# A two-layer GELU network with its gradients on one core: three moves in the order of TensorE's products

## The chip, the cores and the metric

The kernel runs on one core of one Trainium2 chip. The metric is the device time of one execution in microseconds; the time before is 266.73 us, the median of 3 runs (266.65 to 266.77). Profiles are of one execution each. The engines are TensorE (PE, matrix products; PEld is its loading of weights), VectorE (DVE), ScalarE (ACT), GpSimd (POOL) and SyncE (SP, which only issues transfers here).

## The reference

The forward pass of a dense layer, a GELU and a second dense layer, and the gradients of all five inputs for a given gradient of the output, in bf16 with S = 2048 rows, D = 448 and F = 1792:

```python
B, S, D, F = 1, 2048, 448, 1792
def _fwd_reference(x, w1, b1, w2, b2):
    h = jnp.einsum("bsd,df->bsf", x, w1) + b1
    h = _gelu(h)                                # tanh form
    return jnp.einsum("bsf,fd->bsd", h, w2) + b2

def reference(x, w1, b1, w2, b2, grad_out):
    _out, _vjp = jax.vjp(_fwd_reference, x, w1, b1, w2, b2)
    return (_out, *_vjp(grad_out))
```

## The kernel before

**Names.** u is x·w1 + b1 before the GELU, h the GELU of it, q = grad_out·w2ᵀ (the gradient that reaches h), gh = q times the slope of the GELU. All of them are held transposed, F on the partitions. An output row tile ("unit") is either of kind o, h·w2 + b2 for 128 rows, or of kind x, gh·w1ᵀ for 128 rows, the gradient of x. The gradients of the weights are xᵀ·gh (w1) and hᵀ·grad_out (w2), that of the biases are sums over rows.

**Tiling.** The 2048 rows are four blocks of 512, F is seven pairs of two 128-wide tiles, so there are 28 steps (block, pair). A step makes u for a pair (`PU[f]`, two PSUM banks), later q for a pair (`PQ[k]`, a pair of banks), and in between ScalarE and VectorE work out h and gh. D = 448 is three full tiles of 128 and a rest of 64. A unit is 14 products of 128 rows by 448 columns, summed over F.

**Two halves of the array.** From the third u on, nearly all products are made by `half_product` (line 265) as products of 64 rows: `side_by_side` issues them in pairs, one on the lower and one on the upper 64 rows of the array, into two different banks. Each pair of full tiles is thus gone through twice: once with the lower rows of the one bank and the upper rows of the other ("first half"), then the other way round ("second half"). When a bank is taken up by the other half of the rows, `half_product` makes TensorE wait until the last product of the first half on that bank is done, unless an earlier wait covers it. `u_of` and `q_of` give the six products of a half, `u_tail` and `q_tail` the products with the rest of 64 rows, `units_side(uns, second, tiles)` the unit products of two units side by side: two for each tile, 28 for all.

**The stages.** (1) The first u's with full 128-row products (L244, L505), after 11 warm-up products (L190). (2) Single steps i = 1 to 11 (the loop at line 556): each issues the u of step i+2, the q of step i, and slices of units between their halves, in the order that the list `between` gives. u of every single step goes into banks 0 and 1 (`open_u`), which ScalarE's `copy_u` (L345) must have emptied before. (3) Double steps, n = 0 to 7 (the loop at line 646): each takes two q's (ks) and prepares two u's (nxt). On TensorE it issues the rests of the u's and q's (`pe_tails`), then `pe_q_rows` (the six-product groups of both q's and the first half of the odd u), then what the diff changes: the first half of the even u around the first half of two units, then the second half of the units, then the second halves of both u's. On VectorE it issues the GELU's slope (`dve_gate`) with the evictions of finished units in the middle of it, then gh (`dve_gh`, L403); on ScalarE the tanh (L363), evictions of x units (L441), copies of u, square (L354) and GELU (L351). (4) The last units (to 177 us). (5) The weight gradients: w1's full tiles (`gw1_full`, L782, 128x128 of the array), w1's rests (`gw1_tail`, L793: two column halves of the array, 128x64), then w2's (`gw2_tile`, L814, 128x128).

**What sets the order.** The program is written in a manual schedule: each engine executes its instructions in the order in which the functions issue them; semaphores between engines are added from the reads and writes of the tiles. PSUM has eight banks: four single ones (`order_a`) and two pairs, two0 and two1. In the double steps q of an even number opens in two0 and of an odd number in two1 (`open_q`), and the two units of a step open in two1 (`open_two(1, 2)`) once gh has read the odd q from there. They must be evicted (`evict`: VectorE L443 for o, ScalarE L441 for x, then a store issued by GpSimd) before the next odd q opens, and `pe_tails` of the next step starts with that odd q, each q product behind a u rest.

Of the kernel before, what the change touches and what calls it, by code (L numbers as in the profile page):

```python
# [19 lines left out]
def kernel(  # L20
# [180 lines left out]
    def cols(p, a):  # L201
        return slice((2 * FP[p] + a) * P, (2 * FP[p] + a + 1) * P)
# [105 lines left out]
    def side_by_side(one, other, part=slice(0, None)):  # L308
        for lo, hi in list(zip(one(LOW), other(HIGH)))[part]:
            half_product(*lo)  # L310
            half_product(*hi)

    def u_of(f, a, first=False):
        b, p = divmod(f, NPAIR)
        return lambda hf: [(("u", f, a), PU[f][a][:], w1_f[hf, kt, cols(p, a)], xT[b][hf, kt, :], hf, first and kt == 0, False)
                           for kt in range(KF)]
# [206 lines left out]
    uns = [open_units[0:2], open_units[2:4]]  # L523
# [6 lines left out]
    def two_units(banks):  # L530
        for n in banks:
            open_unit(one_bank(n, "ps")[:, 0:D])
        return open_units[-2:]

    def fill(part):
        if isinstance(part, tuple):
            part = [(part[0], part[1], t) for t in part[2]]
        for uns, second, t in part:
            units_side(uns, second, [t])

    def tiles(p):
        return range(2 * p, 2 * p + 2)
# [12 lines left out]
    act_gelu([2])  # L555
    for i in range(1, NSINGLE):
        f = i + LEAD
        if i < 6:
            between = [(uns[1], False, tiles(i)), (uns[0], True, tiles(i)[:1]), (uns[0], True, tiles(i)[1:]), (uns[1], True, tiles(i))]
        elif i == 6:  # L560
            between = [(uns[0], True, tiles(i)), (uns[1], False, tiles(i)[:1]), (uns[1], False, tiles(i)[1:]), (uns[1], True, tiles(i))]
        else:
            if i == 7:
                ahead, later = xs, two_units((2, 3))
                slots = [(ahead, False, t) for t in range(6, NF - 2)] + [(later, False, t) for t in range(4)]
                slots += [(ahead, False, t) for t in range(NF - 2, NF)] + [(later, False, t) for t in range(4, NF)]
                slots += [(ahead, True, t) for t in range(NPAIR)] + [(later, True, t) for t in range(NF)]
                slots += [(ahead, True, t) for t in range(NPAIR, NF)]
            between = [slots[2 * c:2 * c + 2] for c in range(5)]
            del slots[0:10]  # L570
        open_u(f)
        open_q(i)
        if i == 1:
            fill(between[0])
        side_by_side(u_of(f, 0, True), u_of(f, 1, True))
        if i > 1:
            fill(between[0])
        else:
            fill(between[1])
        side_by_side(u_of(f, 1), u_of(f, 0))  # L580
        if i > 1:
            fill(between[1])
        pe_tail_pair(f, i, 1)
        pe_tail_pair(f, i, 0)
        fill(between[2])
        side_by_side(q_of(i, 0), q_of(i, 1))
        fill(between[3])
        side_by_side(q_of(i, 1, True), q_of(i, 0, True))
        if i < 6:
            units_side(uns[0], False, tiles(i + 1))  # L590
        elif i > 6:
            fill(between[4])
        if i > 1:
            act_tanh([i])
        if i == 6:
            evictions(2)
        copy_u(f, "aa")
        if i == NSINGLE - 1:
            evictions(2)
        act_square([f])  # L600
        if i == NSINGLE - 1:
            evictions()
        act_gelu([f])
        if i == 1:
            dve_chain("both 1", "cubic 2", "gate 1", "cubic*u 2", "slope 2", "gh 1", "slope*h 2", "cubic 3")
        elif i < NSINGLE - 1:
            dve_chain(f"both {i}", f"cubic*u {i + 1}", f"gate {i}", f"slope {i + 1}", f"gh {i}", f"slope*h {i + 1}", f"cubic {f}")
        else:
            dve_chain(f"both {i}", f"cubic*u {i + 1}", f"gate {i}", f"slope {i + 1}", f"slope*h {i + 1}", f"gh {i}",
                      f"cubic {f}", f"cubic*u {f}", f"slope {f}", f"slope*h {f}")  # L610
        if i == 6:
            evictions()
            open_two(1, 2)
            xs = open_units[-2:]
            units_side(xs, False, range(0, 6))
        if i == 9:
            nc.gpsimd.dma_start(out=g_low[0:DL, :], in_=gT[1][DL:P, 0, :])
            g_swap[1] = g_low
        if i < 8 or i % 2:
            traffic(i if i < 8 else (i + 7) // 2)  # L620
        if i > 6:
            stores(2, f - 1)
# [23 lines left out]
    for n in range(nq):  # L646
        i = 10 + n
        k = NSINGLE + 2 * n
        ks = [k, k + 1]
        fs = [k + 2, k + 3] if k + 2 < NSTEP else []  # L650
        nxt = [k + 4, k + 5] if k + 4 < NSTEP else []
        if n == 0:
            evictions()
        act_tanh(ks)
        if n > 0:
            dve_gate(ks, evictions)
        if n == 0:
            pe_u_rows(fs)
        if fs:
            pe_tails(fs if n == 0 else fs[::-1], ks[::-1])  # L660
        for f in fs[::-1]:
            copy_u(f, "aa")
        pe_q_rows(ks, nxt)
        if n == 0:
            a_ = part_a(ks)
            nc.vector.tensor_scalar(out=a_, in0=a_, scalar1=1.0, scalar2=math.sqrt(0.5), op0=ALU.add, op1=ALU.mult)
            dve_chain(f"tanh {k + 1}", f"gate {k + 1}", f"tanh {k}", f"gh {k + 1}", f"gate {k}", f"gh {k}")
        else:
            for q in ks[::-1]:
                dve_gh(q)  # L670
        ahead = 1 if n else 2
        if nxt:
            open_u(nxt[0])
            side_by_side(u_of(nxt[0], 0, True), u_of(nxt[0], 1, True), slice(0, ahead))
            open_two(1, 2)
            uns = open_units[-2:]
            units_side(uns, False)
            side_by_side(u_of(nxt[0], 0, True), u_of(nxt[0], 1, True), slice(ahead, None))
            units_side(uns, True)
            side_by_side(u_of(nxt[1], 1), u_of(nxt[1], 0))  # L680
            side_by_side(u_of(nxt[0], 1), u_of(nxt[0], 0))
        elif fs:
            uns, held = two_units(order_a[2:4]), two_units(order_a[0:2])
            units_side(uns, False)
            units_side(held, False)
            pe_tails([], [k + 2, k + 3])
            units_side(uns, True)
        if fs:
            act_square(fs)
            act_gelu(fs)  # L690
            dve_cubic(fs)
        if i == 15:
            nc.gpsimd.dma_start(out=g_low[DL:P, :], in_=gT[3][0:DL, 0, :])
            g_swap[3] = g_low
        traffic(i)
        stores(3, k + 1)
# [4 lines left out]
    for banks in (order_a[2:4], None, order_a[0:2], order_a[2:4]):  # L701
        if banks is None:
            open_two(0, 2)
            uns = open_units[-2:]
        else:
            uns = two_units(banks)
# [81 lines left out]
    def gw1_tail(ft0, n):  # L788
        ps = bank_w()
        for st_ in range(NS):  # L790
            b, j = PLACE[st_]
            for h in range(2):
                nc.tensor.matmul(ps[h * DL:(h + 1) * DL, 0:n * P], lhsT=x_nat[:, st_, KF * P:D],  # L793
                                 rhs=gh_nat[:, b, ft0 + h * n:ft0 + (h + 1) * n, j, :], start=(st_ == 0), stop=(st_ == NS - 1),
                                 tile_position=(0, h * DL), skip_group_check=True)
        o = stg.tile([P, SB], BF16, name="st", tag="st")
        nc.scalar.copy(out=o[:, 0:n * P], in_=ps[:, 0:n * P])
        for h in range(2):
            t0, t1 = ft0 + h * n, ft0 + (h + 1) * n
            while t0 < t1:  # L800
                t2 = t0 + 1
                while t2 < t1 and f_at(t2) == f_at(t2 - 1) + P:
                    t2 += 1
                c0 = (t0 - ft0 - h * n) * P
                queued.append(nc.scalar.dma_start(out=out_2[KF * P:D, f_at(t0):f_at(t0) + (t2 - t0) * P],
                                                  in_=o[h * DL:(h + 1) * DL, c0:c0 + (t2 - t0) * P]))
                t0 = t2

    def gw2_tile(ft, halves):
# [8 lines left out]
            queued.append(nc.scalar.dma_start(out=out_4[ft * P:(ft + 1) * P, h * w:(h + 1) * w], in_=o[:, 0:w]))  # L818
        return done

    for ft0, n in ((0, 4), (4, 4), (8, 4), (12, 2)):
        for kt in range(KF):
            gw1_full(ft0, n, kt)
            emit_sum(3)
        if ft0 == 12:
            gw1_tail(0, 4)
            gw1_tail(8, 3)
    for ft in range(NF):
        last = gw2_tile(ft, 2 if ft == NF - 1 else 1)
        if ft + 4 < NF:  # L830
# [35 lines left out]
```

## Time and profile before

| | |
|---|---|
| median of 3 runs | 266.73 us |
| the profiled execution, its time | 267.09 us |
| its span, first to last instruction | 265.3 us |
| TensorE products | 2171, busy 261.6 us |
| VectorE, ScalarE, GpSimd busy | 174.8, 137.4, 42.7 us |
| single steps, i = 1 to 11 | about 14.7 to 67.4 us |
| double steps, n = 0 to 7 | about 67.8 to 153 us |
| weight gradients | 177.2 to 262.5 us |

TensorE's share of busy time is an upper view, since a product's end is modelled and consecutive products overlap in the records; the starts of the products tell how fast they follow each other. A line of the timeline gives start, duration, engine, line of the kernel, operation, output <- inputs, shape and count; instructions that follow each other are merged into one line with their count. "[0.72 <-PE ps L265]" behind a line is the idle time of the engine before it and what ended it. A product of 64 rows is shown as 64*128.

### The profile page before, as it was taken

To read this page: it belongs to the slowest core of one execution; us is meant where nothing else is said; L and a number is where in the kernel's file an instruction comes from. 1 tells how busy PE (TensorE), PEld (TensorE's weight loads), DVE (VectorE), ACT (ScalarE), POOL (GpSimd) and SP (SyncE) were. 2 spreads that over 40 slices of the span, in tenths; PEclk is the share of its full clock that TensorE was granted. 3 is DMA by queue.
4 is the path that set the end of the run, shared out by engine and by line. 5 is a ranking of instruction groups with operands and counts; after the bars stand their busy time and mean duration, and the time that the engine had idled before them with its cause. 6 is when DMAs were issued, how large, how long until landed. Compare 5 with 4: busy or idle time off the path is not lost.

```text
span 265.3 us, 5207 instructions
## 1 busy us (share of the span) xinstructions
PE 261.6 (99%) x2171; PEld 148.9 (56%) x2171; DVE 174.8 (66%) x217; ACT 137.4 (52%) x164; POOL 42.7 (16%) x54
## 2 busy tenths in 40 slices
PE   8999999999999999999999999999999999999995
PEld 3444444444466565555658888864444765555554
DVE  1599999999998978769897731129999991000000
ACT  2799997887997686877749410022111111121111
POOL 1003003300302021010311111220700008900000
PEclk9999999999999999999999999999999999999999
DMA  7999999999999999465381359999211102999851
GB/s 177 234 239 197 215 216 153 227 101 259 282 220 193 248 206 268 89 171 110 95 161 49 67 125 308 349 164 276 81 40 40 49 22 56 212 216 224 203 129 35
DMA packets 111511, 44.47 MB, mean 168 GB/s; under 512 B 91104, under 2 KB 110272, under 8 KB 111488
## 3 DMA queue, kind: packets, MB, share of 16 engines
q1 hardware_dynamic: 104256, 35.79, 65.3%
q0 software_dynamic: 1984, 4.65, 7.2%
q10 hardware_dynamic: 5248, 3.71, 4.7%
q8 instruction: 17, 0.28, 0.4%
q14 instruction: 6, 0.05, 0.1%
HBM read 7.23 MB, written 14.23 MB: 81 GB/s over the span
## 4 chain that ended last, share of the span: by engine, by line
PE 99%; ACT 0%; issue 0%
PE ps L265 32%; PE ps_v L814 16%; PE pu L265 16%; PE pq L265 15%; PE ps_w L782 14%; PE ps_w L793 2%; PE pw L190 2%; PE pu L244 2%; PE pu L505 0%; PE ps L431 0%; ACT st L817 0%
## 5 line engine op out<-in xcount | busy, mean ns | idle before, releaser
L265 PE MATMUL pq<-gT,w2T 64*128 64x512 bf16 x386 | 55.6, 376 | 0.0
L265 PE MATMUL ps<-w_sb,hT 64*128 64x448 bf16 x440 | 49.0, 349 | 0.0
L265 PE MATMUL ps<-w1T_sb,ghT 64*128 64x448 bf16 x448 | 48.8, 349 | 0.0
L345 ACT ACTIVATE U<-pu,b1T 128x512 bf16<-128x512 f32 x54 | 33.5, 688 | 18.9 <-PE pu L265 14.4
L814 PE MATMUL ps_v<-g_nat,h_nat 128*128 128x448 bf16 (+1 forms) x240 | 42.6, 340 | 0.0
L403 DVE SCALAR_TENSOR_TENSOR ghT<-AZ,pq 128x1024 bf16<-128x1024 bf16 x28 | 33.9, 1218 | 12.3 <-PE pq L265 11.8
L265 PE MATMUL pu<-xT,w_f 64*128 64x512 bf16 x300 | 41.4, 376 | 0.0
L444 POOL DMA_DIRECT2D out_dram<-st x32 | 19.8, 625 | 133.3 <-DVE st L443 70.9
L265 PEld LDWEIGHTS <-ghT 64*128 64x128 bf16 x448 | 28.9, 94 | 15.3
L782 PE MATMUL ps_w<-gh_nat,x_nat 128*128 128x512 bf16 (+1 forms) x192 | 36.5, 352 | 0.0
L265 PEld LDWEIGHTS <-hT 64*128 64x128 bf16 x440 | 26.4, 94 | 17.0 <-issue 0.5
L265 PEld LDWEIGHTS <-w2T 64*128 64x128 bf16 x392 | 26.4, 94 | 14.9 <-PE pq L265 1.0
L814 PEld LDWEIGHTS <-h_nat 128*128 128x128 bf16 x240 | 23.3, 98 | 19.3 <-DMA out_dram<-st 0.3
L363 ACT ACTIVATE AZ<-AZ 128x1024 bf16<-128x1024 bf16 (+1 forms) x20 | 27.8, 1391 | 6.8 <-DVE AZ L359 6.8
L768 DVE TENSOR_TENSOR acc<-acc,gh_nat 128x1792 f32<-128x1792 f32 x14 | 30.0, 2142 | 0.5
L782 PEld LDWEIGHTS <-x_nat 128*128 128x128 bf16 x192 | 18.7, 98 | 17.9 <-issue 0.4
L354 ACT ACTIVATE AZ<-U 128x1024 bf16<-128x1024 bf16 (+1 forms) x21 | 28.2, 1342 | 0.9 <-DVE U L347 0.4
L351 ACT ACTIVATE hT<-U 128x1024 bf16<-128x1024 bf16 (+1 forms) x22 | 28.0, 1277 | 0.0
L817 ACT CAST st<-ps_v 128x448 bf16<-128x448 f32 (+1 forms) x15 | 7.6, 507 | 34.8 <-PE ps_v L814 34.8
L265 PEld LDWEIGHTS <-w_f 64*128 64x128 bf16 x300 | 16.2, 94 | 15.0 <-issue 0.7
L441 ACT CAST st<-ps 128x448 bf16<-128x448 f32 x16 | 7.8, 539 | 29.3 <-PE ps L265 27.6
L785 ACT CAST st<-ps_w 128x512 bf16<-128x512 f32 (+1 forms) x12 | 6.4, 532 | 27.7 <-PE ps_w L782 27.7
(58 smaller groups left out, 192.2 us busy)
## 6 DMA issues: line engine op xcount, KB each, us to landing
hT_dram<-hT SPq DMA_DIRECT2D x28, 256.0 KB, 3.2
out_dram<-st POOLq DMA_DIRECT2D x32, 112.0 KB, 4.7
x_nat<-in_x_dram SPq DMA_DIRECT2D x1, 1792.0 KB, 10.2
g_nat<-in_grad_out_dram SPq DMA_DIRECT2D x1, 1792.0 KB, 15.6
out_dram<-st ACTq DMA_DIRECT2D x13, 112.0 KB, 3.3
out_dram<-st ACTq DMA_DIRECT2D x9, 128.0 KB, 1.7
w_f<-in_w_dram SPq DMA_DIRECT2D x5, 192.0 KB, 3.8
w_sb<-in_w_dram SPq DMA_DIRECT2D x3, 224.0 KB, 3.8
```

The lines of the kernel that those rows point to most:

```text
L265: mm = nc.tensor.matmul(ps, lhsT=w, rhs=m, start=start, stop=stop, tile_position=(hf.start, 0), skip_group_check=True)
L345: nc.scalar.activation(out=dst, in_=PU[f][a][:], func=ACT.Identity, bias=bias)
L351: nc.scalar.activation(out=rows(hT, r), in_=part_u(r), func=ACT.Gelu_apprx_tanh)
L354: nc.scalar.activation(out=part_a(ks), in_=part_u(ks), func=ACT.Square, scale=math.sqrt(3.0 * GELU_A * GELU_C))
L363: nc.scalar.activation(out=z, in_=z, func=ACT.Tanh, scale=-1.0 / 3.0)
L403: nc.vector.scalar_tensor_tensor(out=rows(ghT, [k]), in0=part_z([k]), scalar=1.0, in1=PQ[k][:], op0=ALU.subtract if single else ALU.add, o ...
L441: nc.scalar.copy(out=st[:, 0:D], in_=self.ps)
L444: pooled.append(nc.gpsimd.dma_start(out=(out2 if self.kind == "o" else gx2)[r:r + P, :], in_=st[:, 0:D]))
L768: last_sum[:] = [nc.vector.tensor_tensor(out=v, in0=in0, in1=gh_nat[:, b, :, j, :], op=ALU.add)]
L782: nc.tensor.matmul(ps[:, 0:n * P], lhsT=x_nat[:, st_, kt * P:(kt + 1) * P], rhs=gh_nat[:, b, ft0:ft0 + n, j, :], start=(st_ == 0), stop=(s ...
L814: nc.tensor.matmul(ps[:, 0:w], lhsT=h_nat[ft][:, st_, :], rhs=g_nat[:, st_, h * w:(h + 1) * w], start=(st_ == 0), stop=(st_ == NS - 1))
L817: done = nc.scalar.copy(out=o[:, 0:w], in_=ps[:, 0:w])
```

## The change

Three edits, all of them in the order of issue.

In the first single step (i = 1) the list `between` is dealt out anew: before, four unit products stood ahead of u's first half, two between the halves of u, two behind the rests, four between the halves of q. After, six stand ahead of u, two between its halves, two behind the rests, two between the halves of q.

In the double steps all six products of the even u's first half go ahead of the units (before: two of them, four in the first double step, and the others between the units' halves), and the odd u's second half goes between the units' halves (before: behind both).

The two `gw1_tail` calls go from behind the last `gw1_full` to ahead of the first.

```diff
@@ first single step
         f = i + LEAD
-        if i < 6:
+        if i == 1:
+            between = [(uns[0], True, tiles(1)[1:]), None, (uns[1], True, tiles(1)[:1]), (uns[1], True, tiles(1)[1:])]
+        elif i < 6:
             between = [(uns[1], False, tiles(i)), (uns[0], True, tiles(i)[:1]), (uns[0], True, tiles(i)[1:]), (uns[1], True, tiles(i))]
...
         if i == 1:
-            fill(between[0])
+            units_side(uns[1], False, tiles(1))
+            units_side(uns[0], True, tiles(1)[:1])
         side_by_side(u_of(f, 0, True), u_of(f, 1, True))
-        if i > 1:
-            fill(between[0])
-        else:
-            fill(between[1])
+        fill(between[0])
         side_by_side(u_of(f, 1), u_of(f, 0))
@@ double steps
-        ahead = 1 if n else 2
         if nxt:
             open_u(nxt[0])
-            side_by_side(u_of(nxt[0], 0, True), u_of(nxt[0], 1, True), slice(0, ahead))
+            side_by_side(u_of(nxt[0], 0, True), u_of(nxt[0], 1, True))
             open_two(1, 2)
             uns = open_units[-2:]
             units_side(uns, False)
-            side_by_side(u_of(nxt[0], 0, True), u_of(nxt[0], 1, True), slice(ahead, None))
+            side_by_side(u_of(nxt[1], 1), u_of(nxt[1], 0))
             units_side(uns, True)
-            side_by_side(u_of(nxt[1], 1), u_of(nxt[1], 0))
             side_by_side(u_of(nxt[0], 1), u_of(nxt[0], 0))
@@ weight gradients
+    gw1_tail(0, 4)
+    gw1_tail(8, 3)
     for ft0, n in ((0, 4), (4, 4), (8, 4), (12, 2)):
         for kt in range(KF):
             gw1_full(ft0, n, kt)
             emit_sum(3)
-        if ft0 == 12:
-            gw1_tail(0, 4)
-            gw1_tail(8, 3)
```

## The prediction

> **What bounds the kernel now.** I read the page's busy shares and slices first, then the chain of waits, then the timeline at each place that the change touches, engine beside engine.
>
> The page: busy time by engine, and the clock granted to TensorE in 40 slices.
>
> ```profile
> PE 261.6 (99%) x2171; PEld 148.9 (56%) x2171; DVE 174.8 (66%) x217; ACT 137.4 (52%) x164; POOL 42.7 (16%) x54
> ...
> PEclk9999999999999999999999999999999999999999
> ```
>
> TensorE (PE) is never out of work for long and its clock is full, so the time is the sum of its products plus the few places where the next product has to wait. Moving products about can only gain or lose at such places. The chain of waits, in order of time, gives the prices of the pieces that are moved (start, us, what):
>
> ```profile
> 84.80 0.65 PE pu L265 x6
> ...
> 86.31 2.65 PE ps L265 x28
> ```
>
> Six u products (three pairs, one on each half of the array's rows) take 0.65 us, so a pair takes 0.216; 28 unit products (14 pairs) take 2.65, so a pair takes 0.19.
>
> The place that matters is the seam between two double steps. There the two units of a double step end, are evicted from the bank pair two1, and the next q of odd number opens in two1. Here is TensorE at one of the six seams, then VectorE (DVE) at the same time:
>
> ```profile
> 91.29 0.74 PE L265 MATMUL ps<-w_sb,hT 64*128 64x448 bf16 x6
> 91.86 1.47 PE L265 MATMUL pu<-xT,w_f 64*128 64x512 bf16 x12
> 93.16 0.38 PE L265 MATMUL pu<-xT,wt 64*128 64x512 bf16 x1
> 93.29 0.37 PE L265 MATMUL pq<-gT,w2T 64*128 64x512 bf16 x1
> ```
>
> ```profile
> 91.38 0.69 DVE L372 TENSOR_SCALAR AZ<-AZ 128x2048 bf16<-128x2048 bf16 x1
> 92.08 1.16 DVE L443 TENSOR_TENSOR st<-ps,b_bc 128x448 bf16<-128x448 f32 x2
> 93.15 0.68 DVE L375 TENSOR_SCALAR AZ<-AZ 128x2048 bf16<-128x2048 bf16 x1
> ```
>
> The reader is to see a relay. The units' last product hands over to the first u product at 91.86; the two evictions start 0.22 later (92.08) and end at 93.24; the q product starts 0.05 after that (93.29). It is 0.13 behind the u rest (93.16) that it should run beside. So from the end of the units' issue to the first q product at least 0.22 + 1.16 + 0.05 = 1.43 us must pass, and 12 u products (1.30 us) lie in between as cover. The three other seams with VectorE evictions have the same: u products at 80.42, 126.00, 137.45, first q product at 81.83, 127.43, 138.88, that is 1.41, 1.43 and 1.43. At the two seams where the units are of the x kind ScalarE (ACT) evicts:
>
> ```profile
> 103.31 1.47 PE L265 MATMUL pu<-xT,w_f 64*128 64x512 bf16 x12
> 104.61 0.38 PE L265 MATMUL pu<-xT,wt 64*128 64x512 bf16 x1
> 104.62 0.38 PE L265 MATMUL pq<-gT,w2T 64*128 64x512 bf16 x1
> ```
>
> ```profile
> 103.53 0.97 ACT L441 CAST st<-ps 128x448 bf16<-128x448 f32 x2 [0.72 <-PE ps L265]
> ```
>
> There the relay needs 0.22 + 0.97 + 0.05 = 1.24 us, the cover of 1.30 is just enough, and the q product starts with its u rest (104.62 and 104.61). The bracket says that ScalarE had idled 0.72 for the units: nothing but their end sets the start of the evictions. The other such seam (u at 114.66, evictions 114.88 to 115.85, q at 115.97) is the same.
>
> **The change, part by part.** No product, eviction or transfer is added or removed; only TensorE's order changes, and with it the order of ScalarE's last copies and their DMAs.
>
> *Double steps.* Per step the order was: 2 products of the even u (4 in the first step), 28 unit products, the other 4 (2), 28 unit products, 6 of the odd u, 6 of the even u. It becomes 6, 28, 6 of the odd u, 28, 6 of the even u. The units end six products later, and only six u products, 0.65 us, are left between their end and the q products. The relay is as long as before, because its start is the units' end and its pieces are unchanged. So the first q product waits 1.43 - 0.65 = 0.78 us in place of 0.13 at a VectorE seam, and 1.24 - 0.65 = 0.59 in place of nothing at a ScalarE seam. Both evictions must be over, not the first alone: in the instruction order of both programs that q product waits for the count that the second eviction reaches. TensorE issues in order, so behind it stand the other rests, the six-product groups of both q's and the next u; nothing can fill the hole. Sum: 4 x 0.65 + 2 x 0.59 = **+3.78 us**.
>
> What becomes late next: VectorE has L375 and L376 behind its evictions, then L403 (the gradient of h), which the next units need for their bank. At the seam above L403 started at 96.30 after waiting 1.20 us for the q products, and the evictions' end still comes 0.05 ahead of the q product, so the same 1.20 remains: 0. ScalarE's copies of u also waited for TensorE (2.27 us at this seam): 0.
>
> On the gain side, the units of a double step started right behind their two u products, as soon as L403 was done; in four of the six steps one half of the rows waited 0.04 to 0.11 us there (at 86.12, for example, where two u products started at 85.82). In the timeline only the half that was ahead lost that, while the other ran through, so I count it as nothing; if it were all real, 0.04 + 0.09 + 0.10 + 0.11 = 0.34 us. In the first double step two u products alone stood between the units' halves and the second half waited for the first half's bank (77.76 after products at 77.45): the half that was behind lost 0.02. With six products between, no such wait: **-0.02**.
>
> *The step with i = 1.* ScalarE's two copies of the third u must free banks 0 and 1 before the fourth u opens there. ScalarE, then TensorE:
>
> ```profile
> 14.13 1.25 ACT L345 ACTIVATE U<-pu,b1T 128x512 bf16<-128x512 f32 x2
> ```
>
> ```profile
> 14.67 0.54 PE L265 MATMUL ps<-w_sb,hT 64*128 64x448 bf16 x4
> 15.05 1.19 PE L265 MATMUL pu<-xT,w_f 64*128 64x512 bf16 x6
> 15.88 0.55 PE L265 MATMUL ps<-w_sb,hT 64*128 64x448 bf16 x2
> 16.29 0.82 PE L265 MATMUL pu<-xT,w_f 64*128 64x512 bf16 x6
> ```
>
> The second copy ends at 15.38; six u products that should fill 0.65 start at 15.05 and give way at 15.88. One more unit pair ahead of them (0.19) goes into that wait. The u's second half at 16.29 waits for the last product of its first half on the same bank; with the first half still held by the copy, it starts at 16.30 either way. So 0.19 is gained, and at the other end of the step only one unit pair is left between the q's halves where there were two. The nearest rows are the first q's in the trace (rests at 12.14 to 12.36, next group 0.04 late, both halves restarting in step): a loss of 0.03 to 0.05. Net **-0.15**; bounds -0.19 (no such loss) and 0 (the second copy's end found late elsewhere). ScalarE's next copies end at 19.37, and the next u starts at 19.65 less 0.15, so nothing takes it back.
>
> *The rests of w1's gradient first.* The array's shape changes from 64 rows to 128x128 to 128x64 and back; now it goes from 64 rows to 128x64 to 128x128.
>
> ```profile
> 176.19 1.11 PE L265 MATMUL ps<-w1T_sb,ghT 64*128 64x448 bf16 x9
> 177.23 1.04 PE L782 MATMUL ps_w<-gh_nat,x_nat 128*128 128x512 bf16 x4
> ```
>
> ```profile
> 218.75 1.14 PE L793 MATMUL ps_w<-gh_nat,x_nat 128*64 128x384 bf16 x12
> 219.83 0.74 PE L814 MATMUL ps_v<-g_nat,h_nat 128*128 128x448 bf16 x3
> ```
>
> Each change of shape costs 0.09 to 0.10: the last unit product starts at 176.95 and the first product of L782 at 177.23, 0.28 against 0.19; the rests end with 0.26 against 0.16; into the rests it is 0.20 against 0.11. One change of three is saved: **-0.09**, bounds -0.10 and, if the change from 64 rows straight to 128x64 costs two, 0. The first rest reads all its columns of gh_nat and x_nat some 36 us sooner; gh_nat's last transpose was issued by 157.08 and landed at most 11.9 later (169), x_nat 10.2 after 158.82 (169): done 8 us before. ScalarE's two copies and five DMAs move with them, into a stretch where its copies idle 27.7 us in all: 0.
>
> *Sum.* 3.78 - 0.02 - 0.15 - 0.09 = +3.52. The profiled execution took 267.09 (span 265.3 and 1.8 around it), 0.36 above the median 266.73; its stalls are differences inside the span, so they carry over to the median: 266.73 + 3.5 = 270.2.
>
> **Rivals.**
> (a) *Only VectorE's seams stall*: ScalarE has idled 0.72 before its casts, and if its relay were shorter than the rows say, the two 0.59 fall away: 266.73 + 2.60 - 0.26 = 269.1. Against: the cast pair's 0.97 alone exceeds 0.65.
> (b) *The stall counts twice*: a later gate makes L403 late for the next units, another 0.65 at four steps: 270.2 + 2.6 = 272.8. For: VectorE is busy some 9 tenths here. Against: the 1.20 us that L403 waits.
> (c) *Hidden anyway, not slower*: a later wait of TensorE swallows all of it. The place would be the start of the weight gradients at 177.23, if they were held by x_nat, gh_nat or h_nat; it decides if such a load arrived 3.5 us or more after TensorE was ready. Then only the gains count: 266.73 - 0.26 = 266.5. Against: both landings at 169 and a gap of 0.09 at 177.23 that a change of shape explains.
> (d) *The clock drops*: six holes of 0.6 to 0.8 us could cost TensorE its clock. At the start 11 products of 512 columns took 4.85 us (0.44 each against 0.216), and with the slow stretch up to about 6.6 us half of 5.8 was lost, 2.9; six times that makes 270.2 + 17.4 = 287.6. Against: the clock stayed full over the hole of 0.38 at 15.05.
> The Trainium skill ("TensorE: Matmul & The Clock Gate", section "A second HAM failure mode: psum-queue depth-cycling") says that frequent micro-idles between groups of products can make the clock swing between half and full. By that rule (d) would be the case; this trace has small holes at every seam and a full clock, and speaks against it.
> (e) *The change does not do what it says*: the instruction order shows the three moves as written, so I give it nothing.
>
> **From there to the numbers.** Chances: forecast 0.84, (a) 0.06, (b) 0.05, (c) 0.03, (d) 0.01, rest 0.01. The bounds of the unknown costs are -0.34, -0.19 and -0.10 on one side and 0 in place of the 0.26 on the other: 269.9 to 270.5. Small errors in six relays (0.05 each) and a part of (a) and (b) widen this to 269.2 to 271.2. Faster or slower is told beyond 0.2%, 0.53 us: slower 0.95, within it 0.02, faster 0.03.
>
> **What would show it.** In the changed profile the stretch from the last group of u products to the first pq product grows to about 1.4 us at four seams and 1.24 at two, with one u rest issued and TensorE empty behind it; a double step lasts 0.6 us longer, the steps up to 67 us end 0.15 earlier, and L791 follows the units with one change of shape fewer. The forecast falls if the pq products start within 0.2 us of their u rest, or if TensorE waits somewhere else.

## The result, and the profile after

The changed kernel takes 270.53 us (median of 4 runs, 270.15 to 271.0) beside 266.70 before: ratio 1.0144, 95% interval 1.0127 to 1.0162. Run once more on another occasion it took 270.58 beside 266.93, ratio 1.0132 (1.0118 to 1.0146). The forecast was 270.2. The profiled execution took 271.0, the longest of the four, with a span of 269.2. The page, first and third line:

```profile
span 269.2 us, 5202 instructions
...
PE 261.9 (97%) x2171; PEld 137.5 (51%) x2171; DVE 174.9 (65%) x217; ACT 137.7 (51%) x164; POOL 43.2 (16%) x54
```

The same 2171 products have nearly the same busy time (261.9 against 261.6), but TensorE's share is 97% where it was 99%: it now waits. Where, the timeline of the seam shows that stood at 91.29 to 93.29 before; TensorE first, then VectorE:

```profile
93.28 0.38 PE L265 MATMUL pu<-xT,w_f 64*128 64x512 bf16 x1
...
93.47 0.81 PE L265 MATMUL pu<-xT,w_f 64*128 64x512 bf16 x5
93.92 0.38 PE L265 MATMUL pu<-xT,wt 64*128 64x512 bf16 x1
94.89 0.37 PE L265 MATMUL pq<-gT,w2T 64*128 64x512 bf16 x1 [0.59 <-DVE st L443]
94.89 0.39 PE L265 MATMUL pu<-xT,wt 64*128 64x512 bf16 x1
95.10 0.37 PE L265 MATMUL pq<-gT,w2T 64*128 64x512 bf16 x1
...
95.32 0.38 PE L265 MATMUL pq<-gT,w2T 64*128 64x512 bf16 x1
```

```profile
93.68 1.16 DVE L443 TENSOR_TENSOR st<-ps,b_bc 128x448 bf16<-128x448 f32 x2 [0.65 <-PE ps L265]
94.75 0.68 DVE L375 TENSOR_SCALAR AZ<-AZ 128x2048 bf16<-128x2048 bf16 x1
```

The relay is as it was: u products at 93.47, evictions 0.21 later, 1.16 long, the q product 0.05 behind their end, 1.42 in all. But there are six u products in it and not twelve. They would be through at 93.47 + 0.65 = 94.12; the q product starts at 94.89, 0.77 later. (Its first u rest, on the other half of the rows, had started another 0.2 earlier, since the halves run out of step here.) VectorE now idles 0.65 for the units' end, where it had none before. At a ScalarE seam, TensorE, then ScalarE:

```profile
105.58 0.81 PE L265 MATMUL pu<-xT,w_f 64*128 64x512 bf16 x5
106.03 0.38 PE L265 MATMUL pu<-xT,wt 64*128 64x512 bf16 x1
106.80 0.37 PE L265 MATMUL pq<-gT,w2T 64*128 64x512 bf16 x1 [0.40 <-ACT st L441]
```

```profile
105.78 0.97 ACT L441 CAST st<-ps 128x448 bf16<-128x448 f32 x2 [1.37 <-PE ps L265]
```

106.80 - 105.58 - 0.65 = 0.57 of waiting. The other four seams of this trace give 0.76, 0.57, 0.77 and 0.76 in the same way. Over the double steps, 75 to 150 us, the view of waits counts them (total, times, longest); neither of the last two lines exists in the profile of before:

```profile
DVE ghT L403 <- PE pq L265: 9.8, 6, 2.8
...
PE pq L265 <- DVE st L443: 2.1, 4, 0.6
PE pq L265 <- ACT st L441: 0.8, 2, 0.4
```

Four and two seams, as foretold. The view counts only the time in which nothing ran on TensorE, 2.9 us; while the one half of the rows already waits, the other is still at its last u products, and that part of the wait is not in the count. The first line says that L403, behind the later evictions, still waits for TensorE. And the chain of waits between 90 and 98 us, all TensorE before, now passes through the evictions:

```profile
90.98 2.68 PE ps L265 x25
...
93.68 1.17 DVE st L443 x2
...
94.89 0.37 PE pq L265
```

The changed first single step, and the changes of the array's shape:

```profile
15.06 0.81 PE L265 MATMUL pu<-xT,w_f 64*128 64x512 bf16 x6
15.71 0.35 PE L265 MATMUL ps<-w_sb,hT 64*128 64x448 bf16 x2
15.94 0.82 PE L265 MATMUL pu<-xT,w_f 64*128 64x512 bf16 x6
```

```profile
180.22 1.11 PE L265 MATMUL ps<-w1T_sb,ghT 64*128 64x448 bf16 x9
181.26 1.05 PE L791 MATMUL ps_w<-gh_nat,x_nat 128*64 128x512 bf16 x8
```

```profile
222.79 1.15 PE L780 MATMUL ps_w<-gh_nat,x_nat 128*128 128x256 bf16 x9
223.77 0.92 PE L812 MATMUL ps_v<-g_nat,h_nat 128*128 128x448 bf16 x4
```

The u's first half is no longer held (0.65 from 15.06 to 15.71 where it was 0.83 before). Between the last w1 and the first w2 product there is no change of shape any more.

One thing was in no forecast, a hole in the single steps of this execution:

```profile
44.89 0.38 PE L265 MATMUL pq<-gT,w2T 64*128 64x512 bf16 x1
45.89 0.55 PE L265 MATMUL ps<-w1T_sb,ghT 64*128 64x448 bf16 x4 [0.62 <-DMA w1T_sb<-in_w_dram]
```

1.00 us between two products that were 0.22 apart before: a tile of w1T landed at 45.85, 0.04 before the product that reads it; in the profile of before it landed at 41.79. The table splits the time by the distance between the starts of the same two products in each trace, in us. Where the two halves of the rows are a little apart, the later one is taken; differences are taken before rounding.

| from, to | before | after | after, second profile |
|---|---|---|---|
| the second of q 0's rests, first u product of step i = 2 | 7.29 | 6.94 | 6.94 |
| on to the odd u of the first double step (74 us) | 54.04 | 54.88 | 54.04 |
| on to the q's of the seventh double step (141 us) | 67.35 | 71.05 | 71.06 |
| on to the last unit product | 35.91 | 35.91 | 35.91 |
| last unit product to w2's gradient | 42.88 | 42.79 | 42.79 |

The third row is the loss, +3.70 and +3.71. The six waits account for it: together 4.20, less the 0.13 that each of the four VectorE seams lost before, is 3.68. The second row has the hole, 0.83 more, in the first profile and nothing in the second. The last row is -0.10.

### The profile page after: what moved, and what is told of

The parts are those of the page before. It is cut to its first block, busy times and chain, and to the rows that moved or that the text cites. A ratio compares the mean times of both kernels' runs of the same rounds, so it can differ in the third digit from the quotient of the medians.

```text
span 269.2 us, 5202 instructions
## 1 busy us (share of the span) xinstructions
PE 261.9 (97%) x2171; PEld 137.5 (51%) x2171; DVE 174.9 (65%) x217; ACT 137.7 (51%) x164; POOL 43.2 (16%) x54
## 3 DMA queue, kind: packets, MB, share of 16 engines
q10 hardware_dynamic: 5248, 3.71, 4.6%
## 4 chain that ended last, share of the span: by engine, by line
PE 79%; SPq 14%; DMA 2%; DVE 1%; issue 1%; ACT 1%
PE ps L265 26%; PE ps_v L812 16%; PE ps_w L780 14%; PE pq L265 13%; PE pu L265 8%; SPq L134 4%; SPq L113 3%; PE ps_w L791 2%; DMA w1T_sb<-in_w_dram 2%; SPq L180 2%; DVE st L443 1%; SPq L120 1%; SPq L136 1%; SPq L103 1%; SPq L130 1%
## 5 line engine op out<-in xcount | busy, mean ns | idle before, releaser
L265 PE MATMUL pq<-gT,w2T 64*128 64x512 bf16 x386 | 56.4, 376 | 3.0 <-DVE st L443 2.1
L265 PE MATMUL ps<-w1T_sb,ghT 64*128 64x448 bf16 x448 | 50.2, 349 | 0.6 <-DMA w1T_sb<-in_w_dram 0.6
L265 PE MATMUL ps<-w_sb,hT 64*128 64x448 bf16 x440 | 50.1, 349 | 0.0
L265 PE MATMUL pu<-xT,w_f 64*128 64x512 bf16 x300 | 44.3, 377 | 0.0
L403 DVE SCALAR_TENSOR_TENSOR ghT<-AZ,pq 128x1024 bf16<-128x1024 bf16 x28 | 33.9, 1218 | 14.2 <-PE pq L265 13.7
L265 PEld LDWEIGHTS <-ghT 64*128 64x128 bf16 x448 | 24.1, 94 | 21.0 <-issue 0.9
L265 PEld LDWEIGHTS <-hT 64*128 64x128 bf16 x440 | 24.5, 94 | 18.7 <-issue 0.4
L265 PEld LDWEIGHTS <-w2T 64*128 64x128 bf16 x392 | 23.6, 94 | 20.3 <-PE pq L265 0.9
L265 PEld LDWEIGHTS <-w_f 64*128 64x128 bf16 x300 | 18.0, 94 | 15.4 <-PE pu L265 0.3
```

The source lines that it names most:

```text
L265: mm = nc.tensor.matmul(ps, lhsT=w, rhs=m, start=start, stop=stop, tile_position=(hf.start, 0), skip_group_check=True)
L403: nc.vector.scalar_tensor_tensor(out=rows(ghT, [k]), in0=part_z([k]), scalar=1.0, in1=PQ[k][:], op0=ALU.subtract if single else ALU.add, o ...
```

## The experiments

All are timed in five rounds beside the kernel before on the same chip; ratios are to that, and they are not the quotients of the two medians, from which they differ by up to 0.0016.

**The edits one by one.** The double-step edit alone, the edit of i = 1 alone, the moved rests alone, and the two small edits together: each is the hunk of the diff above, applied to the kernel before.

> The kernel before with the double-step edit alone. My theory (six u products fewer between the units' end and the next odd q): +3.8 us on the kernel before, about 270.5, with the pq products 0.78 us behind their u rest at four seams and 0.59 at two. Rival: the changed kernel's loss has another source (a transfer that lands late in the single steps): then this alone costs clearly less than 3.8, and the other edits cost something.

Measured 270.57, ratio 1.0152 (1.0130 to 1.0174), +3.64 over 266.93. Its profile has the six waits and no hole near 45 us, and the third row of the table reads 71.06, as in the changed kernel. The loss is this edit's; the rival falls.

> The kernel before with the edit of the step i = 1 alone. My theory: -0.15 us, 266.55, with nothing given back later. Rival: TensorE, ahead by 0.15, runs into a transfer that lands later (w1T's tiles near 45 us, where the changed kernel's profile shows a hole): then the same or slower, with a spread between runs that the kernel before does not have.

> The kernel before with the rests of w1's gradient moved to the front alone. My theory: -0.09 us, 266.6, one change of the array's shape fewer. Rival: a change from 64-row products straight to 128x64 costs as much as two: 266.7, no change.

> Both small edits, the double steps as before. My theory: -0.24 us, 266.45. Rival (the late transfer): no gain or up to 0.8 us slower in some of the runs.

Measured 266.86, 266.78 and 266.62 beside 266.93: ratios 1.0004 (0.9992 to 1.0016), 0.9995 (0.9976 to 1.0014) and 0.9995 (0.9985 to 1.0005). None of the three is told from no change by its time. The traces are sharper: the last row of the table is 42.79 in every profile with the moved rests and 42.88 in every one without, and the first row is 7.11 to 7.29 in the four profiles with the old first step and 6.94 to 7.15 in the nine with the new one, 0.21 less on the mean, though the two ranges touch. Neither gain is lost between there and the end in the traces: the rows in between are equal to 0.01. The late transfer was in none of these three profiles.

**The relay made shorter.** If evictions hold the q product, their length must show. First, one of the two units to each engine (a plain copy on the engine that does not have it by its kind; one unit of each o pair thus comes out without b2):

```diff
-            un.evict()
+            un.evict(split and m_ == 1)
```

> The changed kernel, but of the two units that end in a double step one is evicted by VectorE and the other by ScalarE, side by side. (One unit of each pair of the o kind comes out without b2, so that ScalarE can copy it.) My theory: the relay shortens from 0.22 + 1.16 + 0.05 to 0.22 + 0.62 + 0.05 = 0.89 at the VectorE seams and to about the same at the others, stalls of 0.24 in place of 0.78 and 0.59, so 2.9 us less than the changed kernel, about 267.7. Rival: the q products wait for something other than the evictions (an order on TensorE, a transfer): no change, 270.5.

Measured 271.27, ratio 1.0164 (1.0149 to 1.0179): not faster than the changed kernel but, by its third row, slower, against my expectation. Its timeline says why:

```profile
93.03 0.62 DVE L445 TENSOR_TENSOR st<-ps,b_bc 128x448 bf16<-128x448 f32 x1 [0.65 <-PE ps L265]
...
93.69 0.53 ACT L441 CAST st<-ps 128x448 bf16<-128x448 f32 x1 [2.02 <-DVE st L445]
...
94.27 0.37 PE L265 MATMUL pq<-gT,w2T 64*128 64x512 bf16 x1 [0.62 <-ACT st L441]
```

The two evictions don't run side by side. The second waits for the first, across the engines (ScalarE's cast is released by VectorE's eviction, and at a ScalarE seam the other way round), though they read different banks of the pair. Both banks are one tile in the program; that the wait comes from this is likely, but not shown. So the experiment didn't shorten the relay. It lengthened it, to 0.62 + 0.53 with a hand-over between where ScalarE alone took 0.97, and the third row of the table rose to 71.63, as the theory has it for a longer relay. The expectation failed on what the edit does, and as a test it was weak.

So the evictions were shortened on their own engine, by leaving half of their columns out (only columns 0 to 223 are copied and stored):

```diff
-            dve_gate(ks, evictions)
+            dve_gate(ks, lambda: evictions(w=D // 2))
```

> The changed kernel, but each of the units that end in a double step has only the first 224 of its 448 columns evicted and stored (the other half of these output columns is left out). The evictions stay on the one engine, so they can't be put one behind the other across engines as in the run with the split evictions. My theory: the pair takes some 0.6 to 0.7 us in place of 1.16 on VectorE and of 0.97 on ScalarE, stalls of about 0.3 and 0.25 in place of 0.78 and 0.59: 2.4 to 2.7 us less than the changed kernel, about 268.0. Rival: the stall is not the evictions' length but a fixed time of handing over between the engines: less than 0.5 us gained, 270.

Measured 267.90, ratio 1.0036 (1.0023 to 1.0048), 2.7 under the changed kernel; third row 68.51. VectorE, then TensorE:

```profile
92.67 0.69 DVE L443 TENSOR_TENSOR st<-ps,b_bc 128x224 bf16<-128x224 f32 x2 [0.65 <-PE ps L265]
```

```profile
92.46 0.81 PE L265 MATMUL pu<-xT,w_f 64*128 64x512 bf16 x5
92.91 0.38 PE L265 MATMUL pu<-xT,wt 64*128 64x512 bf16 x1
93.41 0.39 PE L265 MATMUL pq<-gT,w2T 64*128 64x512 bf16 x1
```

0.47 shorter evictions, and the q product comes 0.95 behind the u products in place of 1.42: microsecond for microsecond. (The stores are half as long too, but the q product still starts 0.05 behind the end of the evictions, so it is these that it follows.)

**The cover made longer, in two ways.** First the banks: from one double step to the next the two pairs change places, so that the odd q, first in the order, no longer opens where the units were.

```diff
-        PQ[k] = two_banks(0 if k < NSINGLE else order_b[k % 2], "pq")
+        PQ[k] = two_banks(0 if k < NSINGLE else order_b[(k + k // 2) % 2], "pq")
...
-            open_two(1, 2)
+            open_two(order_b[(k + 1 + (k + 1) // 2) % 2], 2)
```

> The changed kernel, with the two pairs of banks of the double steps exchanged from one step to the next, so that the odd q, which comes first, opens in the pair that no units used, and the even q, two pairs of products later, in the one that they leave. My theory: two pairs (0.43 us) more cover, stalls of 0.35 at four seams and 0.16 at two in place of 0.78 and 0.59: 2.58 us less than the changed kernel, about 268.0. Rival: the first q product waits for another thing than its bank: no change, 270.5.

Measured 267.97, ratio 1.0043 (1.0029 to 1.0056); third row 68.47, 2.59 under the changed kernel's where 2.58 was expected.

```profile
93.27 0.38 PE L265 MATMUL pq<-gT,w2T 64*128 64x512 bf16 x1
...
93.48 0.38 PE L265 MATMUL pq<-gT,w2T 64*128 64x512 bf16 x1
...
94.03 0.37 PE L265 MATMUL pq<-gT,w2T 64*128 64x512 bf16 x1 [0.16 <-DVE st L443]
```

The odd q's two rests run on time, 0.21 apart. The even q's first one, which now opens in the units' banks, comes 0.55 behind, 0.34 too late. The wait follows the bank and not the place in the order.

Second, the changed order with only two of the odd u's six products between the units' halves:

```diff
-            side_by_side(u_of(nxt[1], 1), u_of(nxt[1], 0))
+            side_by_side(u_of(nxt[1], 1), u_of(nxt[1], 0), slice(0, 1))
             units_side(uns, True)
+            side_by_side(u_of(nxt[1], 1), u_of(nxt[1], 0), slice(1, None))
```

> The changed kernel, but of the odd u's second half only two products stand between the units' halves and four behind them: ten products of cover (1.08 us). My theory: the same stalls as in the run with the banks exchanged, 0.35 and 0.16, by another way, and 0.02 in each step for the units' second half, which now waits for its bank: about 268.1. Rival: what costs is the odd u between the units as such (the order of the halves), then any part of it costs the whole: 270.5.

Measured 267.97, ratio 1.0040 (1.0028 to 1.0053); third row 68.61.

```profile
91.97 1.24 PE L265 MATMUL pu<-xT,w_f 64*128 64x512 bf16 x10
93.05 0.38 PE L265 MATMUL pu<-xT,wt 64*128 64x512 bf16 x1
93.38 0.37 PE L265 MATMUL pq<-gT,w2T 64*128 64x512 bf16 x1
```

Ten products of cover, a wait of 0.33. Putting the odd u between the halves is not dear as such; what is dear is what it takes away behind them, product by product: four products more, 0.43 us by their price, shorten the wait from 0.77 to 0.33.

**A version under both kernels.** The kernel before lost 0.13 at its four VectorE seams. The exchanged banks give it 0.43 more cover. With both small edits, and alone:

> The kernel before with the two small edits and the exchanged banks: 1.30 + 0.43 = 1.73 us of cover against a relay of 1.43. My theory: the 0.13 that the kernel before still loses at four seams is gone too: 0.5 less than with the small edits alone, about 266.1, under both kernels. Rival: another wait (L403's for the units' start) takes the place of the one removed: no better than the small edits alone, 266.6.

> The kernel before with nothing but the exchanged banks. My theory: the four stalls of 0.13 go, -0.5 us, 266.4 beside 266.95. Rival: the gain of the kernel with both small edits and exchanged banks came mostly from the small edits: -0.2 or less.

Measured 266.13 beside 266.97, ratio 0.9973 (0.9962 to 0.9983), and 266.60 beside 266.93, ratio 0.9986 (0.9977 to 0.9996). In both profiles the third row is 66.88 to 66.89, 0.47 under the kernel before. The first version, VectorE, then TensorE:

```profile
91.55 1.15 DVE L443 TENSOR_TENSOR st<-ps,b_bc 128x448 bf16<-128x448 f32 x2
```

```profile
91.34 1.46 PE L265 MATMUL pu<-xT,w_f 64*128 64x512 bf16 x12
92.64 0.38 PE L265 MATMUL pq<-gT,w2T 64*128 64x512 bf16 x1
92.64 0.38 PE L265 MATMUL pu<-xT,wt 64*128 64x512 bf16 x1
```

The q product starts at 92.64, exactly 1.30 after the u products, while the evictions still run until 92.70.

**The changed kernel once more.**

> The changed kernel once more, for its spread and for the hole near 45 us in its first profile. If that hole (a transfer of w1T that landed 4 us later than in the profile of before) belongs to the change, it is here again and the double-step edit costs 0.8 less than the whole. If it is chance, this profile has no hole there and the time is some 0.25 below the double-step edit alone, 270.3.

Measured 270.58 (270.37 to 270.61). No hole: the tile of w1T landed at 43.30. In the 12 profiles other than the first of the changed kernel it landed between 41.79 and 43.76, ahead of TensorE's need (45.1 to 45.6); only the 45.85 of that one came after it. So the hole is one execution's chance. The time of 270.3 that went with this reading was not met, though: in the medians this kernel is no faster than the double-step edit alone (270.58 and 270.57), and their ratios, 1.0132 and 1.0152, have intervals that overlap. The small gains, 0.3 together in the traces, are as large as what the start varies: TensorE reached the first u product of step i = 2 between 19.16 and 19.71 us in the 13 profiles. In ten of them the first q rest started 0.05 us after the first tile of w2T had landed (11.88 to 12.37), so this landing moves the start.

## Why the prediction came true, step by step

*The relay and its cover* (+3.78). Right in mechanism, place and size: 0.76 to 0.77 and 0.57 waited per seam where 0.78 and 0.59 were worked out; the stage grew by 3.71 against 3.78 - 0.02 = 3.76. Longer and shorter relays and longer covers moved the time as the same sum says.

*That nothing else becomes late.* Right: L403's wait for q grew, from 8.6 to 9.8 us in the six steps, so VectorE has as much slack as before; and the stage behind the double steps took 35.91 us in all profiles. Rival (b) falls with it, (a) falls by the two ScalarE waits, (c) by the third row having come through to the end.

*The wait for L403 at the units' start, counted as nothing.* Right: had the 0.34 been real, the stage would have grown by some 3.4 and not 3.71. The reason came out only with the exchanged banks: there the units follow the two u products without a wait in all but the first double step,

```profile
96.74 0.38 PE L265 MATMUL pu<-xT,w_f 64*128 64x512 bf16 x2
96.95 1.68 PE L265 MATMUL ps<-w1T_sb,ghT 64*128 64x448 bf16 x16
```

0.21 apart, although no product was put ahead of them. In the kernel before, the steps behind a VectorE seam show that wait and those behind a ScalarE seam, which loses nothing, do not. A step of each kind:

```profile
97.26 0.51 PE L265 MATMUL pu<-xT,w_f 64*128 64x512 bf16 x2
97.58 0.38 PE L265 MATMUL ps<-w1T_sb,ghT 64*128 64x448 bf16 x2
```

```profile
108.71 0.39 PE L265 MATMUL pu<-xT,w_f 64*128 64x512 bf16 x2
108.93 0.36 PE L265 MATMUL ps<-w1T_sb,ghT 64*128 64x448 bf16 x2
```

So the idle time there (0.32 between starts against 0.22) was an echo of the seam's 0.13, which had set the two halves of the rows out of step.

*The step with i = 1* (-0.15, bounds -0.19 and 0). The mechanism was right, the size perhaps a little small: the nine profiles with the new step are 0.21 under the four with the old on the mean, just beyond the bound. But profiles of either kind differ by as much among themselves (by 0.18 and 0.21), and the kernel with this edit alone has 7.15, above one of the old ones; so the size is not settled more closely than that. What the sum left out is that the start varies: the old step is between 0.17 and 0.35 longer than the shortest new one. How the landing of q 0's tile would make this difference is not shown.

*The rests first* (-0.09): 0.10 in the traces, one change of shape of 0.09 to 0.10. The change from 64 rows straight to 128x64 costs no more than the others: 180.22 to 181.26 here, 176.19 to 177.23 before.

*The clock* (rival d). It did not drop, and the products show it: behind each of the six holes the q products follow each other by 0.21 to 0.22 us at once (94.89, 95.10, 95.32 above), the pace of the kernel before (93.29, 93.50, 93.72). The row of the granted clock, on which the prediction leaned, is weaker evidence. In the second profile of the changed kernel it is full in all 40 slices,

```profile
PEclk9999999999999999999999999999999999999999
```

but it reads the same in the kernel before over the first slices too, where 11 products took 4.85 us, and for the first profile of the changed kernel there is no such row. The hole of 0.38 at 15.05 that the prediction named against (d) is a distance between two starts, 0.16 more than a product takes. In the holes here nothing at all ran on TensorE for 0.38 to 0.59 us. The Trainium skill ("TensorE: Matmul & The Clock Gate", section "A second HAM failure mode: psum-queue depth-cycling") tells of a kernel in which frequent micro-idles made the clock swing; idle times of this length, about 12 us apart, did not make it swing here.

*The total.* The rows add up: -0.35 + 3.71 - 0.10 = 3.26 for the stages, and the start varies by more than the small terms. Between medians it was 3.83 and 3.65, against 3.5. The 0.4 to 0.6 by which the medians exceed the rows is not traced to a place. The two profiled executions without the hole took 267.09 and 270.61, and there the 3.52 between them are these rows and a start that came 0.28 later (q 0's second rest at 12.36 and at 12.64). So the forecast came true by its one large term, which the runs show. For the small gains it is no evidence: without them it would have been 270.5, nearer to what was measured.

## What to carry to other kernels

When products are moved on an engine that is never idle, don't ask first what they will hide at their new place, but what they covered at the old one. Write the relay down as a sum (last product to eviction, eviction, eviction to next product) and count the products that lie in it: here, below that number each one taken away cost its full time, and above it each one added was free. If the cover can't be lengthened, change who waits: give the bank that is being emptied to the work that comes second.

## What the runs showed of the hardware that had not been expected

The two halves of the array's rows keep their own lag for tens of microseconds: in the kernel before they come out of the last VectorE seam (138.9 us) 0.13 apart, and the last unit products still start 0.13 apart at 176.82 and 176.95; with the exchanged banks, which leave no wait at the seams, they are less than 0.01 apart there. So a wait that the trace shows on one of them can cost nothing (0.09 to 0.11 at the units' start) or be the shadow of an earlier one. The loads at the start land up to 4 us apart from one execution to another (41.79 to 45.85 for the same tile over the 13 profiles, 43.30 and 45.85 in the two of the changed kernel), so a profile can hold a hole of 0.8 us that the next execution of its kernel doesn't have.
